# Where the first spectral products of the first half keep their operands, one values buffer, and another order of the instructions

## The chip, the core and the metric

The kernel runs on one NeuronCore of a Trainium2 chip. TensorE (PE, with its weight loads PEld) multiplies matrices into the eight PSUM banks; VectorE (DVE), ScalarE (ACT) and GpSimd (POOL) work on elements; SP issues most of the DMAs and POOL those that add to their target. The metric is the device time of one execution in microseconds; the kernel before was run three times, and its median is 233.02 us (232.19 to 233.31).

## What is computed

Two branches share the input x (2048 rows of 640 columns, bf16), and a gate mixes them:

```python
x = A_q
g = sigmoid((x * gate_w).sum(-1, keepdims=True))
# A: a 4-tap causal filter of k times v, then a long convolution by FFT along the 2048 rows
k_shift = sum(k_pad[:, t:t + S] * shift_k[:, ks - 1 - t] for t in range(ks))
kv = k_shift * v
y = irfft(rfft(kv, 2 * S) * rfft(ssm_k, 2 * S))[:S] + kv * ssm_D
a = x * y
# B: a mixer and an MLP
h = gelu(layernorm(x) @ w1)
x1 = x + shifted(h) @ w2              # four column groups, shifted by +1, -1, +2, -2 rows
b = x1 + gelu(layernorm(x1) @ w3) @ w4
out = g * a + (1 - g) * b
```

## The kernel before

All of SBUF that the kernel uses is one array, `arena`, cut into regions by hand (lines 530 to 546), and PSUM is another, `PSall`. Every instruction is recorded as an operation with the byte ranges that it reads and writes; dependencies follow from the ranges. Two long lists then fix the rest: `SEQUENCE` is the order in which the recorded operations are issued (each engine takes its own operations in this order and waits in order), and `PLACES` is the PSUM bank of each PSUM tile. `emit` turns the dependencies into semaphore waits. So an operation that is not ready holds everything behind it on its engine, DMA queues included. In the profile nearly all operations have the line of a recording helper: 646 is every matmul of `mm`, 636 every ACT operation, 626 every tensor_tensor, 631 every tensor_scalar, 238 every plain DMA, 235 every transposing DMA.

The mixer goes by four chunks of 512 rows: `x_load`, `ln1` (layer norm, transposes), `mm1` with gelu into `hT`, `mm2` by tiles of 128 rows, `ln2` (normalise, then a transposing DMA on SP), `mm3` with gelu into `uT` (12 tiles of 5 matmuls of 512 columns), `mm4` (two halves of 12 or 13 matmuls of 320 columns for a tile). `base` scales the residual rows and stores them, and `mm4` overwrites the rows in SBUF and adds them to the output by an accumulating DMA of POOL.

The convolution goes by five chunks of 128 channels. `h_load`, `h_fold`, `h_chunk` bring the filter into the frequency domain, in `HF`. `kv_load` (line 771) brings 128 channels of keys and of values with transposing DMAs, into one key buffer `kT` and one of two value buffers `vT`. `kv_chunk` (line 776) works on DVE: four scalings and three sums for the taps, the product with the values, a reversed copy on ACT, and four folds of 1024 elements; then a transposing DMA writes `xet`. `x_fwd` (line 789) transforms `xet` with 12 matmuls on PE, and ACT copies the result into `XF`, whose first index is the half (channels 0 to 319 and 320 to 639). The first half is complete after chunk 2, the second after chunk 4.

Rows are four blocks of 512. `combine(g, b)` (line 959) makes sums and differences of neighbouring blocks in `XF`: the sum (frequencies 0 and 1 of the four groups) by an accumulating DMA of POOL, the difference on DVE. `unit(hh, c)` (line 965) makes output block c of half hh: products of `XF` block c - a with `HF` block a, for a = 0 to c, each for a real and an imaginary accumulator, as operations of 2560 elements. The products of a = 1 are added by accumulating DMAs, the others on DVE. Two subtractions or sums of 1280 elements a block write the result over `XF`. `final` (line 1004) transforms back with 8 matmuls and one flip on PE, copies on ACT, and finishes on DVE; the result is added to the output by a DMA of POOL or, for the last four, stored by SP.

The buffers of `unit` come from a list, `ubuf` (line 576): regions `oYX` and `oPT` (two), the end of `oHT`, and the end of `oKV`. `oKV`, `oYX` and `oPT` lie behind one another, 15376 elements, and the chunks of keys and values use all of them: keys at 0, the first value buffer at 2064, the taps at 4112 and 6160, the reversed copy at 8208, the second value buffer at 9232, the folds (`xf2`) at 11280 and `xet` at 13328. `G`, the matrix of the back transform, is loaded over the key buffer.

Of the kernel before, what the change touches and what calls it, by code (L numbers as in the profile page):

```python
# [422 lines left out]
def bass_gated_mix__ssm_conv_h3__mixer_s_mlp__prompt_kernel(  # L423
# [32 lines left out]
    def ps(n, cls):  # L456
# [3 lines left out]
    SEQUENCE = [74, 11, 54, 76, 56, 1, 12, 7, 73, 9, 2, 53, 0, 13, 75, 14, 156, 15, 157, 16, 80, 57, 217, 17, 81, 66,  # L460
# [310 lines left out]
    def kv_load(c):  # L771
        cs = slice(128 * c, 128 * (c + 1))
        P.dma(sp, kT[:, 16:16 + S], A_k[0, :, cs], transpose=True)
        P.dma(sp, vT[c % 2], A_v[0, :, cs], transpose=True)
# [190 lines left out]
    def unit(hh, c):  # L965
# [35 lines left out]
        if c == 3:  # L1001
            pool.insert(0, V(oHF + 10240 * hh + 7680, 2560))
# [146 lines left out]
```

## Time and profile before

| What | Before |
|---|---|
| median of three runs | 233.02 us |
| the profiled execution's own time | 234.02 us |
| its span, first to last instruction | 232.2 us |
| PE, DVE, ACT, POOL busy | 218.2, 204.9, 175.4, 91.7 us |
| PEld busy | 128.2 us |
| granted TensorE clock, mean | 0.993 |
| DMA packets, bytes | 81439, 46.00 MB |

Busy times are unions of instructions on one engine; matmuls are pipelined and their ends are modelled, so a busy PE is not PE at its peak, but a gap in it is a wait. A row of a timeline gives the start, the length, the engine, the line, the operation, what it writes and reads, and in brackets the idle time before it with what ended it; instructions of one line that follow each other are merged under the shape of the first. A stretch of the windows view gives start and end, its length, then busy microseconds (and instructions) of PE, PEld, DVE, ACT and POOL, the granted clock, the DMA engines' share and GB/s. Times are microseconds from the span's start.

### The profile page before, as it was taken

What the parts mean: (1) busy time and instruction counts of PE and PEld (TensorE: products, weight loads), DVE (VectorE), ACT (ScalarE), POOL (GpSimd) and SP (SyncE); (2) the same over time, 40 slices, a digit from 0 to 9 for tenths busy, and PEclk for the clock granted to TensorE, in tenths of its full rate; (3) what the DMA queues carried; (4) which work ended last, traced back from release to release, by engine and by line L of the source; (5) the groups of instructions that cost most, each with busy time, mean ns of one, the idle gap of its engine ahead of it and who ended that gap; (6) DMA issues with size and microseconds to landing.
All of it is one profiled execution on the core that took longest, in us unless ns stands there. A gap on an engine that the chain in (4) does not pass through costs nothing.

```text
span 232.2 us, 3873 instructions
## 1 busy us (share of the span) xinstructions
PE 218.2 (94%) x1426; PEld 128.2 (55%) x1437; DVE 204.9 (88%) x336; ACT 175.4 (76%) x315; POOL 91.7 (40%) x114
## 2 busy tenths in 40 slices
PE   7998999999999999987999989999999999999970
PEld 2486866555545634434665437654577554777640
DVE  4999997999799999695556997999999999999993
ACT  2197996796899979987877995458983869446990
POOL 0335140324214000372115814595128634636890
PEclk9999999999999999999999999999999999999997
DMA  6999999999999999999999999999899999899997
GB/s 174 320 233 311 132 247 232 202 203 207 233 142 263 182 229 223 296 210 223 179 203 173 163 163 200 198 189 183 165 249 203 182 224 151 159 173 111 112 138 142
DMA packets 81439, 46.00 MB, mean 198 GB/s; under 512 B 60024, under 2 KB 75916, under 8 KB 81420
## 3 DMA queue, kind: packets, MB, share of 16 engines
q1 hardware_dynamic: 71560, 31.92, 64.5%
q0 software_dynamic: 9696, 13.77, 38.3%
q8 instruction: 11, 0.18, 0.3%
q10 hardware_dynamic: 164, 0.07, 0.1%
q14 instruction: 8, 0.07, 0.1%
HBM read 14.92 MB, written 6.55 MB: 92 GB/s over the span
## 4 chain that ended last, share of the span: by engine, by line
PE 80%; ACT 9%; DMA 5%; DVE 4%; issue 1%
PE PSall L646 74%; ACT arena L636 9%; DMA arena<-arena 5%; DVE arena L626 3%; PE PSall L674 3%; PE PSall L678 2%; PE PSall L865 1%; DVE arena L918 0%; DVE arena L670 0%; PE PSall L709 0%
## 5 line engine op out<-in xcount | busy, mean ns | idle before, releaser
L646 PE MATMUL PSall<-arena 128*128 128x320 bf16 (+5 forms) x1345 | 206.1, 309 | 6.4 <-ACT arena L636 3.1
L646 PEld LDWEIGHTS PSall<-arena 128*128 128x128 bf16 (+1 forms) x1354 | 121.9, 98 | 90.4 <-ACT arena L636 7.5
L626 DVE TENSOR_TENSOR arena<-arena 128x2560 bf16<-128x2560 bf16 (+6 forms) x195 | 158.5, 865 | 13.5 <-DMA arena<-arena 4.7
L636 ACT ACTIVATE arena<-PSall 128x512 bf16<-128x512 f32 (+7 forms) x182 | 104.8, 630 | 23.1 <-PE PSall L646 15.1
L636 ACT ACTIVATE arena<-arena 128x640 bf16<-128x640 bf16 (+4 forms) x75 | 54.0, 747 | 11.0 <-DVE arena L626 6.9
L238 POOL DMA_DIRECT2D out_dram<-arena x28 | 29.3, 1141 | 20.8 <-ACT arena L636 15.5
L238 POOL DMA_DIRECT2D arena<-arena x18 | 20.4, 1131 | 37.7 <-DVE arena L626 23.4
L636 ACT ACTIVATE arena<-PSall,arena 128x640 bf16<-128x640 f32 (+1 forms) x32 | 20.4, 658 | 15.4 <-PE PSall L646 15.2
L814 POOL TENSOR_TENSOR arena<-arena 128x1 f32<-128x1 f32 (+2 forms) x17 | 18.7, 1104 | 29.1 <-DVE arena L825 20.6
L631 DVE TENSOR_SCALAR arena<-arena 128x640 bf16<-128x640 bf16 (+3 forms) x45 | 23.7, 541 | 1.2 <-DMA arena<-arena 0.4
L626 POOL TENSOR_TENSOR arena<-arena 128x4 bf16<-128x4 bf16 (+3 forms) x26 | 15.9, 675 | 21.3 <-DVE arena L626 14.5
L631 POOL TENSOR_SCALAR arena<-arena 128x2 f32<-128x2 f32 (+4 forms) x21 | 11.0, 527 | 25.6 <-DVE arena L811 8.7
L810 DVE BATCH_NORM_STATS2 arena<-arena 128x6 f32<-128x320 bf16 x32 | 14.4, 483 | 2.1 <-DMA arena<-in_A_q_dram 2.0
L918 DVE SCALAR_TENSOR_TENSOR arena<-PSall,arena 128x640 bf16<-128x640 f32 x12 | 9.8, 822 | 3.6 <-PE PSall L646 3.6
L674 PE MATMUL PSall<-arena 128*128 128x512 bf16 x15 | 6.1, 594 | 1.6 <-DVE arena L670 1.6
L678 PE MATMUL PSall<-arena 128*128 128x512 bf16 x24 | 6.6, 379 | 0.0
L674 PEld LDWEIGHTS PSall<-arena 128*128 128x128 bf16 x15 | 2.1, 143 | 5.1 <-issue 3.6
L865 PE MATMUL PSall<-arena 128*128 128x128 bf16 x40 | 3.3, 219 | 0.1
L678 PEld LDWEIGHTS PSall<-arena 128*128 128x128 bf16 x26 | 2.4, 98 | 1.6
L865 PEld LDWEIGHTS PSall<-arena 128*128 128x128 bf16 x40 | 2.7, 98 | 0.6
L636 ACT ACTIVATE PSall<-PSall 128x640 f32<-128x640 f32 x4 | 2.8, 688 | 0.1
L811 DVE BATCH_NORM_AGGREGATE arena<-arena 128x2 f32<-128x12 f32 x16 | 2.7, 192 | 0.0
(26 smaller groups left out, 10.8 us busy)
## 6 DMA issues: line engine op xcount, KB each, us to landing
arena<-arena POOLq DMA_DIRECT2D x12, 640.0 KB, 6.6
arena<-in_A_q_dram SPq DMA_DIRECT2D x14, 320.0 KB, 4.8
out_dram<-arena POOLq DMA_DIRECT2D x20, 160.0 KB, 4.5
arena<-in_A_ssm_k_dram SPq DMA_DIRECT2D x5, 512.0 KB, 5.8
arena<-in_B_w_dram SPq DMA_DIRECT2D x4, 480.0 KB, 4.7
arena<-arena POOLq DMA_DIRECT2D x6, 320.0 KB, 4.5
out_dram<-arena SPq DMA_DIRECT2D x10, 160.0 KB, 4.5
arena<-in_B_w_dram SPq DMA_DIRECT2D x1, 1152.0 KB, 7.0
```

The costliest lines, as they stand in the source:

```text
L238: fn = lambda e: e.dma_start(out, in_, **kw)
L626: P.op(eng, lambda e: e.tensor_tensor(o, real(a), real(b), op), [a, b], [o], dve_ns(o, [a, b], 2) if eng == "dve" else 500)
L631: P.op(eng, lambda e: e.tensor_scalar(o, real(a), s1, s2, op0=op0, **({} if op1 is None else {"op1": op1})), [a] + aps, [o], dve_ns(o, [a] ...
L636: P.op("act", lambda e: e.activation(real(o), real(a), f, bias=bias, scale=scale, **({"accum_out": accum} if accum is not None else {})), ...
L646: fns.append(lambda e, l=l, r=r, i=i: e.matmul(real(o), l, r, start=(i == 0), stop=(i == last)))
L674: P.op("pe", lambda e: e.matmul(real(pw), warm[:, 0:128], warm[:, 128:640], start=True, stop=True), [warm], [pw], 427.0 if i < 14 else 216.0)
L678: P.op("pe", lambda e: e.matmul(real(pw), warm[:, 0:128], warm[:, 128:640], start=True, stop=True), [warm], [pw], 216.0)
L810: P.op("dve", lambda e, o=o, i=i: e.bn_stats(o, i), [i], [o], 400)
L811: P.op("dve", lambda e: e.bn_aggr(bna[:, t, :], bns[k]), [bns[k]], [bna[:, t, :]], 120)
L814: P.op("pool", lambda g: g.tensor_tensor(o, a, e, ALU.pow), [a, e], [o], dur)
L865: P.op("pe", [lambda e, c=c, pb=pb, xn=xn: e.transpose(real(pb)[:, 128 * c:128 * (c + 1)], xn[:, 128 * c:128 * (c + 1)], ident) for c in r ...
L918: P.op("dve", lambda e: e.scalar_tensor_tensor(x, real(pr), 1.0, x, op0=ALU.mult, op1=ALU.add, accum_out=st[1, 0][:, t:t + 1]), [pr, x], [ ...
```

## The change

The regions are used in another way, and the two lists are other ones.

- The chunks of keys and values now lie in the first 12304 elements: one value buffer, the reversed copy over it, the folds at 8208 and `xet` at 10256. So the values load of a chunk must wait until the chunk before has read its reversed copy.
- The first two units of the first half (blocks 3 and 2) take three buffers: the end of `oHT`, `oW2` (the weights of `mm2`, which are spent by then), and the end of the old `oPT` (offset 12816 behind `oKV`), which the chunks do not touch. From unit (0,1) on, three buffers inside `oKV` follow in place of `oW2`, where `final` keeps its results.
- With three buffers, these two units add each product as it comes: a = c down to 1, into one temporary (real part) and into `XF`'s own block (imaginary part), whose values are spent after the first two products. The products of a = 1 are still added by DMA. The number of products and of sums is the same.
- `combine` of the first half makes its sums on DVE in place of POOL's DMA.
- `SEQUENCE` and `PLACES` are others throughout. Around the last two chunks of keys and values the order is now as follows.
  - SP: values of chunk 3, transpose of chunk 2's folds, a part of w4, keys of chunk 4, two parts of w4, an `ln2` transpose, transpose of chunk 3's folds, the last part of w4, an `ln2` transpose, values of chunk 4, two `ln2` transposes, G, seven `base` stores, transpose of chunk 4's folds. Before: values of chunk 3, transpose of chunk 2's folds, two parts of w4, keys of chunk 4, two parts of w4, values of chunk 4, transpose of chunk 3's folds, two `base` stores, two `ln2` transposes, three `base` stores, transpose of chunk 4's folds, and G later.
  - DVE: chunk 3, then chunk 4 with six combine operations and the first three products of unit (0,3) among its own; its other nine products and sums follow at once, then products of units (0,2) and (0,1). Before: chunk 3, chunk 4 with one combine operation of the first half in it, and unit (0,3) behind it.
  - PE: six tiles of `mm3(0)`, `x_fwd(2)`, the other six tiles, nine of the 12 matmuls of `x_fwd(3)`, then `mm4` of tiles 0 to 3 with the other three among them, three tiles of `mm3(1)`, four matmuls of `x_fwd(4)`, nine more tiles of `mm3(1)` with two matmuls of `x_fwd(4)` between the last two, the other six matmuls, and `mm4` of tiles 4 to 7. The first back transforms, of block 3, stand before and after the last half of these, ahead of `mm3(2)`; before, the first ones came after it.
  - At the start the first two tiles of x are loaded in the other order, and the weights of `mm1` earlier.

The diff, without the two lists:

```diff
-    kT, vT = V(oKV, 2064), [V(o, 2048) for o in (oKV + 2064, oKV + 9232)]
+    kT, vT = V(oKV, 2064), V(oKV + 2064, 2048)
     tap = [V(oKV + 4112 + 2048 * i, 2048) for i in range(2)]
-    xrev = V(oKV + 8208, 1024).rearrange("p (b h n) -> p b h n", b=4, h=2)
+    xrev = V(oKV + 2064, 1024).rearrange("p (b h n) -> p b h n", b=4, h=2)
...
-    xf2 = V(oKV + 11280, 2048).rearrange("p (e a b n) -> p e a b n", e=2, a=2, b=4)
-    xet = V(oKV + 13328, 2048).rearrange("p (e b c) -> p e b c", e=4, b=4)
+    xf2 = V(oKV + 8208, 2048).rearrange("p (e a b n) -> p e a b n", e=2, a=2, b=4)
+    xet = V(oKV + 10256, 2048).rearrange("p (e b c) -> p e b c", e=4, b=4)
...
-    ubuf = [V(o, 2560) for o in (oYX, oPT, oPT + 2560, oHT + 7680, oKV + 5120)]
+    first = [V(o, 2560) for o in (oHT + 7680, oW2, oKV + 12816)]
+    later = [V(oKV + o, 2560) for o in (5120, 7680, 10240)]
...
-        P.dma(sp, vT[c % 2], A_v[0, :, cs], transpose=True)
+        P.dma(sp, vT, A_v[0, :, cs], transpose=True)
...
     def combine(g, b):
-        P.dma("pool", XF[:, g, b, 0:2].rearrange("p j r d -> p (j r d)"), XF[:, g, b - 1, 0:2].rearrange("p j r d -> p (j r d)"), accum=True)
+        if g:
+            P.dma("pool", XF[:, g, b, 0:2].rearrange("p j r d -> p (j r d)"), XF[:, g, b - 1, 0:2].rearrange("p j r d -> p (j r d)"), accum=True)
+        else:
+            tt(XF[:, g, b, 0:2], XF[:, g, b, 0:2], XF[:, g, b - 1, 0:2], ALU.add)
         tt(XF[:, g, b, 2:4], XF[:, g, b, 2:4], XF[:, g, b - 1, 2:4], ALU.subtract)
...
-        if c:
+        few = not hh and c > 1
+        if few:
+            T = pool.pop(0)
+            for a in range(c, 0, -1):
+                for o, t, r in ((R, T, 0), (I, Xc, 1)):
+                    prod(t, a, r)
+                    if a > 1:
+                        tt(o, o, t, ALU.add)
+                    else:
+                        P.dma("pool", o.rearrange("p (i n) -> p i n", i=2), t.rearrange("p (i n) -> p i n", i=2), accum=True)
+            pool.append(T)
+        elif c:
...
-        if c > 1:
+        if c > 1 and not few:
...
+        if few and c == 2:
+            pool[:] = later + [b for b in pool if b.offset != first[1].offset]
```

More of the change, by code (lines that the diff above doesn't have):

```diff
@@ L458, in ps @@
         return v if n == 1 else v.rearrange("p (b n) -> p b n", b=2)
[L460 removed]
[59 rows of a table removed]
[L521 removed]
[5 rows of a table removed]
+    SEQUENCE = [76, 11, 56, 74, 54, 9, 1, 12, 75, 5, 4, 53, 7, 13, 8, 0, 73, 10, 14, 156, 15, 157, 16, 57, 60, 17, 81,
[59 rows of a table added]
+    PLACES = [0, 7, 2, 1, 1, 3, 4, 4, 5, 6, 2, 1, 0, 5, 6, 3, 7, 5, 5, 7, 0, 4, 7, 6, 1, 3, 7, 2, 6, 0, 4, 2, 7, 4, 6,
[5 rows of a table added]
     HW = S + 4
@@ L783, in kv_chunk @@
                 tt(kv, kv, dst[j], ALU.add)
-        tt(kv, kv, vT[c % 2], ALU.mult)
+        tt(kv, kv, vT, ALU.mult)
         q = kv.rearrange("p (b h n) -> p b h n", b=4, h=2)
@@ L959, in combine @@
     def combine(g, b):
-        P.dma("pool", XF[:, g, b, 0:2].rearrange("p j r d -> p (j r d)"), XF[:, g, b - 1, 0:2].rearrange("p j r d -> p (j r d)"), accum=True)
+        if g:
+            P.dma("pool", XF[:, g, b, 0:2].rearrange("p j r d -> p (j r d)"), XF[:, g, b - 1, 0:2].rearrange("p j r d -> p (j r d)"), accum=True)
+        else:
+            tt(XF[:, g, b, 0:2], XF[:, g, b, 0:2], XF[:, g, b - 1, 0:2], ALU.add)
         tt(XF[:, g, b, 2:4], XF[:, g, b, 2:4], XF[:, g, b - 1, 2:4], ALU.subtract)
-    pool = list(ubuf)
+    pool = list(first)
     def unit(hh, c):
@@ L1109, in bass_gated_mix__ssm_conv_h3__mixer_s_mlp__prompt_kernel @@
         at(unit, 1, c)
-    spare = sorted((b.offset for b in pool if b.offset in (oYX, oPT, oPT + 2560, oHT + 7680)), key=[b.offset for b in pool].index)[0]
+    spare = sorted((b.offset for b in pool if b.offset in [a.offset for a in first + later[1:]]), key=[b.offset for b in pool].index)[0]
     abl = [V(spare + 640 * i, 640).rearrange("p (e d) -> p e d", e=2) for i in range(4)]
```

1 line of the change is left out of this document (removed), and 128 rows, old and new, of tables (PLACES, SEQUENCE).

## The prediction

> **What bounds the kernel now.** I read the page's busy times and chain first, then TensorE's idle time by stretch, then the timelines of the engines where that idle time lies. The busy times, the DMA slices and the chain by engine:
>
> ```profile
> span 232.2 us, 3873 instructions
> PE 218.2 (94%) x1426; PEld 128.2 (55%) x1437; DVE 204.9 (88%) x336; ACT 175.4 (76%) x315; POOL 91.7 (40%) x114
> ...
> DMA  6999999999999999999999999999899999899997
> ...
> PE 80%; ACT 9%; DMA 5%; DVE 4%; issue 1%
> ```
>
> TensorE (PE) is busy for 94% of the span and is 80% of the chain. The change takes no matmul away, so it can win only what PE waits, plus what follows the last matmul. The 16 DMA engines are busy nearly throughout. Busy time by stretch (start:end, length, then busy us of PE, PEld, DVE, ACT, POOL):
>
> ```profile
> 20.00:30.00 10.00, 8.60 (x95) 7.09 (x94) 9.55 (x23) 9.72 (x29) 4.18 (x7) 1.00 1.22 192
> ...
> 100.00:110.00 10.00, 7.73 (x45) 4.24 (x45) 7.18 (x9) 7.87 (x14) 4.51 (x8) 1.00 1.17 194
> ...
> 120.00:130.00 10.00, 9.73 (x55) 5.13 (x54) 7.51 (x8) 8.07 (x15) 5.64 (x5) 1.00 0.97 195
> 130.00:140.00 10.00, 9.31 (x46) 4.29 (x45) 9.93 (x9) 9.86 (x18) 4.16 (x7) 1.00 0.92 152
> 140.00:210.00 70.00, 70.00 (x447) 43.39 (x446) 68.04 (x71) 46.08 (x83) 36.31 (x33) 1.00 1.01 190
> ...
> 220.00:232.20 12.20, 5.24 (x35) 3.16 (x33) 8.13 (x25) 6.39 (x13) 5.95 (x5) 0.87 0.97 137
> ```
>
> From 140 to 210 PE has no idle time: nothing can be won there, only lost. Between 100 and 140 it idles 2.27 + 0.27 + 0.69 = 3.2 us (110 to 120 has next to none). The early 1.40 us (20 to 30) and the tail after 216 remain. PE's timeline names the middle waits:
>
> ```profile
> 104.53 3.57 PE L646 MATMUL PSall<-arena 128*128 128x320 bf16 x25 [0.69 <-ACT arena L636]
> 109.69 13.12 PE L646 MATMUL PSall<-arena 128*128 128x512 bf16 x82 [1.58 <-DMA arena<-arena]
> 123.08 15.32 PE L646 MATMUL PSall<-arena 128*128 128x512 bf16 x75 [0.27 <-ACT arena L636]
> 139.09 3.16 PE L646 MATMUL PSall<-arena 128*128 128x320 bf16 x22 [0.69 <-ACT arena L636]
> ```
>
> The 1.58 us is `x_fwd` of chunk 3, waiting for the transpose of that chunk's folded values. The 0.69 at 104.53 and at 139.09 are the first `mm4` behind an `mm3`, waiting for the last gelu. VectorE (DVE) idles far more in the same stretch:
>
> ```profile
> 96.42 0.68 DVE L626 TENSOR_TENSOR arena<-arena 128x1024 bf16<-128x1024 bf16 x1
> ...
> 106.45 1.23 DVE L626 TENSOR_TENSOR arena<-arena 128x2048 bf16<-128x2048 bf16 x1 [1.59 <-DMA arena<-in_A_v_dram]
> 108.80 4.88 DVE L626 TENSOR_TENSOR arena<-arena 128x1024 bf16<-128x1024 bf16 x6 [1.12 <-ACT arena L636]
> 118.38 3.02 DVE L626 TENSOR_TENSOR arena<-arena 128x2560 bf16<-128x2560 bf16 x2 [4.70 <-DMA arena<-arena]
> 123.72 2.23 DVE L626 TENSOR_TENSOR arena<-arena 128x2560 bf16<-128x2560 bf16 x2 [2.32 <-PE PSall L646]
> ...
> 144.24 0.16 DVE L825 SCALAR_TENSOR_TENSOR arena<-arena 128x1 f32<-128x1 f32 x1 [1.40 <-ACT arena L636]
> ...
> 173.91 54.55 DVE L626 TENSOR_TENSOR arena<-arena 128x2560 bf16<-128x2560 bf16 x86
> ```
>
> These waits sum to 11.1 us; then DVE runs practically unbroken to 228.46, so it ends the kernel. The 4.70 us is the first product of `unit(0,3)`, whose buffers still held the last chunk's folds until their transpose had read them. That is what the own buffers remove.
>
> **The change part by part.** *DVE.* The units' products and sums are the same number of 2560-element operations as before. Three `combine(0,b)` halves move from POOL's DMA to DVE:
>
> ```profile
> L626 DVE TENSOR_TENSOR arena<-arena 128x2560 bf16<-128x2560 bf16 x52 | 75.4, 1486 | 7.6 <-DMA arena<-arena 4.7 <-PE PSall L646 2.3 <-ACT arena L636 0.2
> L626 DVE TENSOR_TENSOR arena<-arena 128x1280 bf16<-128x1280 bf16 x22 | 17.4, 819 | 0.0
> L626 DVE TENSOR_TENSOR arena<-arena 128x2048 bf16<-128x2048 bf16 x20 | 24.5, 1223 | 1.9 <-DMA arena<-in_A_v_dram 1.6
> L631 DVE TENSOR_SCALAR arena<-arena 128x2048 bf16<-128x2048 bf16 x20 | 14.9, 748 | 0.7 <-DMA arena<-in_A_k_dram 0.4
> ```
>
> That is 3 x 0.82 = 2.5 us of DVE. Against the 11.1 us of waits that early products can fill, DVE could be up to 8.6 us ahead of today from about 145 on. PE cannot follow: its matmuls stay, so DVE's lead is worth only PE's waits and part of the tail. The 2.5 us are hidden by that lead; with the cover gone they would stand in full at the end.
>
> *The third chunk's transpose (1.58 + 0.69 us).* SP and POOL around it:
>
> ```profile
> 91.25 4.15 SPq L235 DMA_TRANSPOSE arena<-in_A_k_dram  x1
> 95.45 1.11 SPq L238 DMA_DIRECT2D arena<-in_B_w_dram  x2
> 96.60 4.94 SPq L235 DMA_TRANSPOSE arena<-in_A_v_dram  x1
> 101.64 4.20 SPq L235 DMA_TRANSPOSE arena<-arena  x1
> ...
> 119.29 1.22 SPq L235 DMA_TRANSPOSE arena<-arena  x1
> ```
>
> ```profile
> 98.22 1.11 POOL L238 DMA_DIRECT2D arena<-arena  x1
> 106.44 0.92 POOL L238 DMA_DIRECT2D arena<-arena  x1 [3.41 <-DMA arena<-arena]
> 111.44 0.91 POOL L238 DMA_DIRECT2D arena<-arena  x1 [3.51 <-DMA arena<-arena]
> ```
>
> ```profile
> arena<-arena POOLq DMA_DIRECT2D x6, 320.0 KB, 4.5
> ...
> out_dram<-arena SPq DMA_DIRECT2D x12, 80.0 KB, 3.1
> ...
> arena<-arena SPq DMA_TRANSPOSE x30, 4.2
> ...
> arena<-in_A_v_dram SPq DMA_TRANSPOSE x5, 6.3
> ```
>
> The folds are done at 96.42 + 0.68 = 97.1, but the transpose stands behind the last chunk's values load and issues only at 101.64; PE gets it at 109.69, 8.05 us later, where the median transpose lands after 4.2. The three accumulating copies of `combine` (98.22, 106.44, 111.44) run beside it and the next one. In the new order the transpose comes before the values load, behind the key load, two weight loads and one small transpose: 91.25 + 4.15 + 1.11 + 1.22 (a small transpose, as at 119.29) = 97.7, so it issues near 98. It lands between 98 + 4.2 = 102.2 and 98 + 8.05 = 106.1. PE now has the rest of `mm3-0` first and needs it where `mm3-0` ends, at 104.53 - 0.69 = 103.8. The wait is 0 to 2.2 us; since the copies beside it are gone I stay near the low end, 0.7. `mm4` then stands behind nine matmuls of `x_fwd`, which cover the gelu wait. Gain: 2.27 - 0.7 = **1.5 us** (bounds 0 to 2.3).
>
> The Trainium skill, page "DMA: Bandwidth & Descriptors", section "Issuing engines are not separate DMA queues", says that transfers of SP and POOL share the same 16 engines and interleave. The 8.05 against 4.2 us agree with it; by that rule taking the copies away brings the low end, without it the transpose keeps 8.05 and the gain here is near nothing.
>
> *The last chunk's transpose.* Between 97.1 and it DVE now has chunk 4 (4 scalings of 0.75, 4 operations of 1.22, 4 folds of 0.68: 10.6), six combine halves (4.9) and three products (4.5): 20.0, so 117.1, with half a microsecond of waits 117.6. It lands at 121.8 to 125.7. PE needs it where it has done chunk 3, four `mm4` and 15 matmuls of `mm3-1`; today `mm3-1` begins 13 matmuls into the burst at 123.08; at 3.57 / 25 = 0.14 us each, near 124.9.
>
> ```profile
> 126.00:137.00 11.00, 11.00 (x53) 1.00 0.96 154
> ```
>
> At 11.00 / 53 = 0.21 us a matmul the 15 add 3.2, the 12 of chunk 4 that are now later take off 2.5, the gains above and the 0.27 take off 1.8: 123.8. The wait is 0 to 1.9; I take 0.5, against today's 0.27: **-0.2 us**.
>
> *The wait at 139.09.* Six matmuls of `x_fwd(4)` now stand between the last `mm3-1` and `mm4-6`, 1.3 us, more than the 0.69 us gelu wait: **+0.7 us**.
>
> *The single values buffer.* The load of chunk c+1 waits for chunk c's second fold, and while it waits it holds all that follows on SP. For chunk 4 it comes behind the transpose, at about 102 to 103, and lands by its median 6.3 us later, at 109; DVE multiplies by it 12.7 us of queue after 97.1 plus some waits, near 110.5. Hidden, by 1.5 us. If it lands like today's (issued at 96.60, DVE released at 106.45, 9.85), it lands at 112.5 and DVE stops for 2 us. The matrix G, which takes the key buffer, stands behind it on SP until DVE has read the keys, near 109, and ahead of the `base` stores, whose rows ACT's `mm4` overwrites. They land 3.1 us later, near 113; the first whole `mm4` tile leaves PE after ten matmuls of `x_fwd(3)` and five halves of 12 or 13, near 104.5 + 2.1 + 61 x 0.14 = 115. Covered by 2 us.
>
> The Trainium skill, page "Trainium Kernel Development and Optimization", section "Best Practices", advises two buffers so that loads overlap computing, which speaks against this edit. Here DVE already waited 1.59 us with two, because the load's place on SP decided; the rule's price is the 2 us above.
>
> *The start.* Tiles, fills and weight loads are reordered. PE's 1.40 us between 20 and 30 can go or double; nothing there is removed, and the first statistics begin on the tile that is now loaded second. I charge **-0.3 us** (bounds -1.4 to +1.4).
>
> *The tail.* DVE's last 12 us stay the same operations. Today it enters them late because it is behind; with the lead PE sets their start. PE's share of the tail stays. I take **+0.2 us** of at most 1.4.
>
> Sum: 1.5 - 0.2 + 0.7 - 0.3 + 0.2 = **1.9 us**. The profiled execution took 234.02, 1.82 more than its span of 232.2 and 1.0 more than the median. Span 230.3, execution 232.1, median 233.02 - 1.9 = **231.1 us**, own range 230.0 to 231.9.
>
> **The rivals.** *Slower: the DMA engines stay the limit.* If the transpose of chunk 3 keeps 8.05 us, it lands at 106.1 and PE waits 2.2, so 1.5 of the gain is lost. The values load comes behind it on SP: 98 + 4.20 + 0.55 of a weight load + 1.22 = 104.0, and 9.85 later it is 113.9. DVE stops from 110.5 on, 3.4 us; the last transpose issues at 117.6 + 3.4 = 121.0 and lands at 129.0, where PE stands at 123.8 + 1.5 = 125.3. That is 3.7 us of wait in place of 0.5: 231.1 + 1.5 + 3.2 = **235.8**. It makes the kernel slower by over 0.5% once the last transpose lands after 127.4. For it: DMA slices of 9 throughout, and the load's own 9.85. Against: the copies are gone from just this stretch.
>
> *Same: the unbroken stretch breaks.* From 140 to 210 PE never waits. The first inverse transforms now stand ahead of `mm3-2`, 60 matmuls or 12.6 us sooner, and `ln2` of the last tile issues its ACT operation only some 36 matmuls of `mm4` (5.0 us) ahead of `mm3-3`:
>
> ```profile
> L636 ACT ACTIVATE arena<-arena 128x640 bf16<-128x640 bf16 x40 | 32.8, 834 | 4.1 <-POOL arena L626 3.6 <-DMA arena<-arena 0.5
> ```
>
> ACT's 0.83, SP's 1.22 and a landing of 4.2 (taken from the issue's start, so 5.0 to 6.3 in all) cost PE 0 to 1.3 us there, and as much again where DVE, ACT and PE hand a transform on: 231.1 + 1.3 + 1.3 = **233.7** at most, 232.4 with one of them. Against it: DVE is ahead there.
>
> *Faster still: all middle waits go and DVE's lead shows in the tail*: 2.3 in place of 1.5, 0.3 in place of -0.2, 0.7, and 1.2 of the tail, less 0.3 at the start, is 4.2: near **228.9**. For it the 11.1 us; against it, every landing must be early.
>
> *It does not do what it says:* the early products wait for ACT's evacuation of `x_fwd(2)`, which the new order mixes with gelus. DVE then gains no lead and carries 2.5 us more: 235.5, within the slower case.
>
> **How the numbers follow.** Forecast 0.42, faster still 0.13, same 0.18, slower 0.27 (0.20 for the DMA case, 0.07 for the products and other waits). About 0.5% (1.2 us) is what a measurement can tell from no change: faster 0.55, same 0.18, slower 0.27. The range 229.0 to 235.0 leaves out the best part of the fast case and the worst of the slow one.
>
> **What would show it.** DVE's 4.70 us wait gone, and products between the folds of chunk 4. The folded transpose of chunk 3 issued near 98 and PE's wait for it under 1 us. No gelu wait ahead of the second block of `mm4`. PE still unbroken from 140 to 210. Wrong, if the last values load holds DVE, if PE waits over 2 us for the last transpose, or if new waits of PE lie before 100.

## The result, and the profile after

The changed kernel takes 231.38 us (median of 20 executions, 230.54 to 235.74) against 233.21 us for the kernel before beside it; the ratio is 0.9935, interval 0.9908 to 0.9962. A second set gave 231.05 against 233.02, ratio 0.9915 (0.9887 to 0.9943). The gain is 1.8 to 2.0 us by the medians and 1.5 to 2.0 by the ratios; 1.9 was forecast. Ratios leave out executions over 1.5% above the fastest of their kernel; medians and ranges do not.

The profiled execution took 233.02 us with a span of 231.2, so it is one of the longer ones; what it has that others lack comes out below. Its busy times:

```profile
span 231.2 us, 3878 instructions
PE 219.1 (95%) x1437; PEld 127.0 (55%) x1437; DVE 206.8 (89%) x339; ACT 175.3 (76%) x315; POOL 96.3 (42%) x111
```

The stretches of the prediction from 100 on, with the same columns:

```profile
100.00:110.00 10.00, 10.00 (x58) 5.51 (x57) 9.97 (x12) 9.77 (x18) 0.00 (x0) 1.00 1.01 200
...
120.00:130.00 10.00, 10.00 (x49) 4.54 (x48) 9.90 (x7) 8.13 (x12) 5.26 (x5) 1.00 0.89 147
130.00:140.00 10.00, 10.00 (x60) 5.52 (x59) 9.75 (x8) 6.88 (x13) 4.79 (x5) 1.00 1.17 190
140.00:210.00 70.00, 67.87 (x429) 41.75 (x428) 65.22 (x74) 48.09 (x85) 40.10 (x36) 1.00 1.00 185
```

From 100 to 140 PE is now busy throughout; before it idled 2.27 + 0.27 + 0.69 = 3.2 us there. All four middle waits are gone. But from 140 to 210, where nothing was lost before, 70.00 - 67.87 = 2.13 us are. PE's timeline has one wait there:

```profile
178.43 36.76 PE L647 MATMUL PSall<-arena 128*128 128x320 bf16 x234 [2.13 <-ACT arena L637]
```

VectorE in the middle, and SP:

```profile
95.53 2.62 DVE L627 TENSOR_TENSOR arena<-arena 128x1024 bf16<-128x1024 bf16 x4 [2.55 <-ACT arena L637]
...
107.72 9.17 DVE L627 TENSOR_TENSOR arena<-arena 128x1280 bf16<-128x1280 bf16 x10
...
117.02 18.68 DVE L627 TENSOR_TENSOR arena<-arena 128x2560 bf16<-128x2560 bf16 x13
```

```profile
94.66 6.39 SPq L235 DMA_TRANSPOSE arena<-arena  x2
...
102.97 2.67 SPq L235 DMA_TRANSPOSE arena<-in_A_v_dram  x1
...
116.96 2.27 SPq L235 DMA_TRANSPOSE arena<-arena  x1
```

Lines of the kernel are one higher than before. DVE's 4.70 us wait is gone, as are the 1.59 for the values and the 2.32 for PE: ten operations run without a gap from 107.72 (a tap sum, the product with the values, folds, combine halves and the early products), and thirteen more from 117.02. On SP the second of the two transposes merged at 94.66 is chunk 3's; it issues at 98.2, the last chunk's at 116.96. The `DMA to landing` line of the source view, for each of them alone:

```profile
L235 SPq DMA_TRANSPOSE arena<-arena x1: 2864/2864/2864, 98.2 to 98.2; - x1
DMA to landing us min/median/max: 4.3/4.3/4.3
```

```profile
L235 SPq DMA_TRANSPOSE arena<-arena x1: 2271/2271/2271, 117.0 to 117.0; - x1
DMA to landing us min/median/max: 4.6/4.6/4.6
```

Both land near the median, and PE waits for neither.

### The profile page after: what moved, and what is told of

It reads as the page before. It is cut to its first block, busy times and chain, and to the rows that moved or that the text cites. A ratio compares the mean times of both kernels' runs of the same rounds, so it can differ in the third digit from the quotient of the medians.

```text
span 231.2 us, 3878 instructions
## 1 busy us (share of the span) xinstructions
PE 219.1 (95%) x1437; PEld 127.0 (55%) x1437; DVE 206.8 (89%) x339; ACT 175.3 (76%) x315; POOL 96.3 (42%) x111
## 4 chain that ended last, share of the span: by engine, by line
PE 77%; ACT 11%; POOL 5%; DVE 4%; issue 2%
PE PSall L647 71%; ACT arena L637 10%; DVE arena L627 3%; POOL arena L627 3%; PE PSall L679 2%; PE PSall L675 2%; POOL arena L238 1%; POOL arena L815 1%; ACT PSall L637 1%; PE PSall L866 1%; DVE arena L919 0%; POOL out_dram L238 0%; DVE arena L671 0%; PE PSall L710 0%
## 5 line engine op out<-in xcount | busy, mean ns | idle before, releaser
L647 PE MATMUL PSall<-arena 128*128 128x320 bf16 (+4 forms) x1354 | 206.1, 310 | 4.9 <-ACT arena L637 3.0
L627 DVE TENSOR_TENSOR arena<-arena 128x2560 bf16<-128x2560 bf16 (+6 forms) x198 | 161.1, 864 | 11.4 <-ACT arena L637 9.6
L647 PEld LDWEIGHTS PSall<-arena 128*128 128x128 bf16 x1354 | 120.5, 98 | 90.5 <-ACT arena L637 10.3
L637 ACT ACTIVATE arena<-PSall 128x512 bf16<-128x512 f32 (+8 forms) x182 | 106.1, 628 | 26.4 <-PE PSall L647 18.2
L238 POOL DMA_DIRECT2D out_dram<-arena x28 | 32.6, 1300 | 46.4 <-ACT arena L637 37.9
L627 POOL TENSOR_TENSOR arena<-arena 128x4 bf16<-128x4 bf16 (+3 forms) x26 | 23.2, 915 | 25.2 <-DVE arena L627 24.5
L238 POOL DMA_DIRECT2D arena<-arena x15 | 22.2, 1490 | 23.9 <-DVE arena L627 23.9
L815 POOL TENSOR_TENSOR arena<-arena 128x1 f32<-128x1 f32 (+2 forms) x17 | 17.9, 1054 | 20.3 <-DVE arena L826 10.8
L632 POOL TENSOR_SCALAR arena<-arena 128x2 f32<-128x2 f32 (+4 forms) x21 | 11.9, 571 | 13.4 <-DVE arena L812 6.1
L675 PE MATMUL PSall<-arena 128*128 128x512 bf16 x15 | 5.5, 551 | 1.6 <-DVE arena L671 1.6
L679 PE MATMUL PSall<-arena 128*128 128x512 bf16 x26 | 6.6, 379 | 0.0
L675 PEld LDWEIGHTS PSall<-arena 128*128 128x128 bf16 x15 | 1.9, 134 | 4.7 <-issue 2.8
L866 PEld LDWEIGHTS PSall<-arena 128*128 128x128 bf16 x40 | 2.6, 98 | 1.3 <-ACT arena L637 0.4
L679 PEld LDWEIGHTS PSall<-arena 128*128 128x128 bf16 x26 | 2.2, 97 | 1.7
```

The lines of the kernel that those rows point to most:

```text
L238: fn = lambda e: e.dma_start(out, in_, **kw)
L627: P.op(eng, lambda e: e.tensor_tensor(o, real(a), real(b), op), [a, b], [o], dve_ns(o, [a, b], 2) if eng == "dve" else 500)
L632: P.op(eng, lambda e: e.tensor_scalar(o, real(a), s1, s2, op0=op0, **({} if op1 is None else {"op1": op1})), [a] + aps, [o], dve_ns(o, [a] ...
L637: P.op("act", lambda e: e.activation(real(o), real(a), f, bias=bias, scale=scale, **({"accum_out": accum} if accum is not None else {})), ...
L647: fns.append(lambda e, l=l, r=r, i=i: e.matmul(real(o), l, r, start=(i == 0), stop=(i == last)))
L675: P.op("pe", lambda e: e.matmul(real(pw), warm[:, 0:128], warm[:, 128:640], start=True, stop=True), [warm], [pw], 427.0 if i < 14 else 216.0)
```

## The experiments

Each kernel ran beside the kernel before on the same chip; the kernel before had medians of 233.02 to 233.26 us there, so medians are compared across chips too. The theory: two things held the transposes back in the kernel before, their place on SP and the copies of POOL beside them; PE's waits there were what could be won, and DVE's early work is cover and no more. The rivals are told with each run.

### The changed kernel again: is the wait at 178 part of it?

No edit.

> The changed kernel once more, without an edit. In its first profile PE waits 2.1 us ahead of mm4 of tile 9 at 178, behind ACT, which waits for one POOL product of 128x1 that took 5.91 us. Theory: that product is stretched now and then by DVE's two-input products beside it, and such executions are the ones near 233.5, the others lie near 231. So an execution near 231 shows the product at 1 to 2 us and no PE wait over 1 us between 140 and 210, and one near 233 shows both again. Rival: the order makes the wait, and POOL's time has nothing to do with it: the wait of about 2 us is there also with the product at 1 us.

It took 231.24 us, span 229.5. Its PE, and its POOL against that of the first profile, around 171:

```profile
84.58 130.71 PE L647 MATMUL PSall<-arena 4*128 4x512 bf16 x781 [0.25 <-issue]
```

```profile
170.87 1.27 POOL L627 TENSOR_TENSOR arena<-arena 128x1 f32<-128x1 f32 x1
```

```profile
170.83 5.91 POOL L627 TENSOR_TENSOR arena<-arena 128x1 f32<-128x1 f32 x1
```

The second fence is this run, the third the first profile: one program, the same instruction, 1.27 and 5.91 us. It is the last product of `ln_math` for tile 15. In the first profile ACT's `ln2` waits for it, and behind `ln2` in ACT's order stands the copy that frees the PSUM bank for the next `mm4`:

```profile
176.78 0.92 ACT L637 ACTIVATE arena<-arena 128x640 bf16<-128x640 bf16 x1 [3.22 <-POOL arena L627]
177.60 0.77 ACT L637 ACTIVATE arena<-PSall,arena 128x640 bf16<-128x640 f32 x1
```

With the product at 1.27 us PE has no wait from 84.58 to 215. The 0.25 us ahead of 84.58 is no wait either: this profile records 1425 matmuls of 1437, and a weight load at 84.25 has no matmul behind it; the first profile, which records all 1437, has that matmul and no gap. So the 2.13 us belong to that execution, not to the order; they are more than the whole 1.78 us between the two times.

### The same product on ACT

```diff
-            tt(s[4], s[2], s[5], ALU.mult, eng="pool")
+            if a < 12:
+                tt(s[4], s[2], s[5], ALU.mult, eng="pool")
+            else:
+                act(s[4], s[2], ACTF.Copy, scale=s[5])   # placed right ahead of its ln2
```

> The changed kernel with the last product of ln_math of tiles 12 to 15 (one element for each partition) on ACT, right ahead of the ACT operation that needs it, in place of POOL. Theory (POOL's product beside DVE's two-input products makes the wait at 178): the wait of 2.1 us is gone, PE is busy for over 69.3 of the 70 us from 140 to 210, the times come in one group near 230.6 to 231.2, and the long group near 233.5 is gone. Rival (ACT's own queue is late there, and POOL is only seen as the releaser): PE still waits 1 to 2 us near 178, and the times are those of the changed kernel. Second rival (POOL's power operation is stretched just as the product was): the wait moves to the power operation and stays over 1 us.

231.07 us (six executions, 230.91 to 231.81), ratio 0.9917 (0.9886 to 0.9947). PE is busy for 70.00 of 70 us from 140 to 210. That agrees with the theory, but the run before has shown that the same holds without the edit. So both kernels were timed once more, side by side.

> The changed kernel without an edit, timed beside the next one, for the share of long executions. Theory: one part near 230.5 to 231.9 and a smaller one (a fifth to a third) from 233 on, as among its first 20 times. Rival (the long ones were chance of that chip): all below 232.5.

> The changed kernel with ln_math's last product of tiles 12 to 15 on ACT once more, for the share of long executions. Theory (the stretched POOL product makes them): no execution above 232.5, median 230.8 to 231.3, 0.2 to 0.6 us below the changed kernel on the same chip. Rival: long executions as often as in the changed kernel; then the POOL product is one way to be late among others.

The changed kernel: 231.05 us (nine, 230.59 to 232.00). With the product on ACT: 231.28 us (seven, 230.74 to 231.86), ratio 0.9914 (0.9883 to 0.9945). No difference. In the first set 6 of 20 executions of the changed kernel lay above 232.5, here none of nine: the rival (chance) held for this chip. So the edit's worth can't be told, and that the stretched product made all the six long ones isn't shown; one profile shows one of them.

### The combine sums by DMA again

```diff
-        if g:
-            P.dma("pool", ...accum=True)
-        else:
-            tt(XF[:, g, b, 0:2], XF[:, g, b, 0:2], XF[:, g, b - 1, 0:2], ALU.add)
+        P.dma("pool", ...accum=True)
```

> The changed kernel with the three sums of combine(0, b) as accumulating DMAs of POOL again, at the same places of the order. Theory (the copies held the transposes back, as the forecast had it): the transposes of the last two chunks land 1 to 4 us later, PE waits 1 to 2.5 us in all between 100 and 125, DVE saves 2.5 us, the time is 1 to 2 us longer than that of the changed kernel. Rival (the place on SP alone did it): the transposes land as in the changed kernel, PE waits under 0.3 us there, and the time is the same within 0.5 us. Either way the first product of unit(0,3) waits for a DMA in place of a DVE instruction, by up to 3.5 us of DVE.

232.55 us (ten, 231.48 to 233.16), ratio 0.9977 (0.9951 to 1.0003): 1.2 us more than the changed kernel by the medians and 1.0 by the ratios, as the theory had it, but not by its way. Chunk 3's transpose issues at 98.2 and lands 4.3 us later, as in the changed kernel, and PE waits 0.46 us between 100 and 125. The first copy issues at 101, behind that transpose, and no longer beside it. What changes is DVE, which waits for a copy in the first product:

```profile
107.55 1.49 DVE L627 TENSOR_TENSOR arena<-arena 128x2560 bf16<-128x2560 bf16 x1 [2.38 <-DMA arena<-arena]
...
118.33 23.00 DVE L627 TENSOR_TENSOR arena<-arena 128x2560 bf16<-128x2560 bf16 x16
```

It is at 118.33 where the changed kernel is at 117.02, 1.3 us later although it has three operations less to do. The profile shows 0.2 to 0.9 us of the 1.2 (span 229.7, against 229.5 and 228.8 of the changed kernel's second and third profiles); it took 231.48, the lowest of the ten, and the rest stays open.

### The values load ahead of the transpose again

```diff
+    SEQUENCE.remove(705); SEQUENCE.insert(SEQUENCE.index(691), 705)   # values of chunk 4 ahead of chunk 3's transpose
```

> The changed kernel with the last chunk's values load put back on SP ahead of the transpose of chunk 3's folds. Theory (that place on SP is what made PE wait): the load must wait for chunk 3's second fold in the single buffer and takes 2.7 to 5 us of SP, so the transpose issues at 100.5 to 103 in place of 98, PE waits 1.5 to 3 us for it near 104, and the time grows by 1 to 2.5 us. Rival (DMA load decides when it lands, the issue does not): the transpose is seen by PE as before and the time stays within 0.5 us.

231.49 us (eight, 230.83 to 232.98), ratio 0.9930 (0.9902 to 0.9959): nothing that can be measured. The load took 3.09 us of SP; the transpose issued at 100.1, 1.9 us later, and landed 4.4 us after that. PE:

```profile
104.51 2.12 PE L647 MATMUL PSall<-arena 128*128 128x512 bf16 x9 [0.26 <-DMA arena<-arena]
106.96 108.21 PE L647 MATMUL PSall<-arena 128*128 128x320 bf16 x677 [0.33 <-issue]
```

0.26 + 0.33 us are lost, where 1.5 to 3 were expected. In the new order the place on SP alone makes PE wait no more than that.

### Both undone

The two edits above, in one kernel:

```diff
+        P.dma("pool", ...accum=True)   # the sums of combine(0, b)
+    SEQUENCE.remove(705); SEQUENCE.insert(SEQUENCE.index(691), 705)
```

> The changed kernel with both undone: the three sums of combine(0, b) by POOL's DMA and the last values load ahead of chunk 3's transpose. Alone, the first cost 1.2 us of time and left that transpose's landing at 102.3, the second cost 0.1 to 0.2 us and moved it to 104.2 with 0.6 us of PE. Theory (each spoils what the other leaves, since a copy now lies beside the transpose): it lands at 105 to 108, PE waits 1.5 to 3.5 us for it, and the time is 2 to 3.5 us longer than that of the changed kernel. Rival (they only add): it lands near 104.2, PE loses 0.6 to 1.1 us there, and the time is 1.2 to 1.6 us longer.

235.55 us (ten, 233.24 to 239.05), ratio 1.0074 (1.0039 to 1.0110). They do not add: 1.2 and 0.1 us alone, 4.2 together by the medians (235.55 - 231.38), 3.2 by the ratios (0.0139 x 233); by the ratios the size is the theory's. The way is not. The transpose lands 4.3 us after 99.7, so at 104.0, and PE does not wait for it. It waits later:

```profile
108.39 115.40 PE L647 MATMUL PSall<-arena 128*128 128x320 bf16 x726 [2.23 <-issue]
```

The instruction at 108.39 is the first `mm4`, which reads all four parts of w4. The last part is the DMA behind the transpose on SP, issued at 101.8 in this run, with a 320 KB copy of POOL issued at 101.2 beside it; in the changed kernel it issues at 101.1 and lands 4.3 us later, at 105.4, before the first `mm4`. By the semaphore events it lands at 108.3 in this run, 6.5 us after its issue, and at 106.9 in the run above, 4.5 us after its issue at 102.35 with no copy beside it; in both the first `mm4` starts within 0.1 us of that. So "issue", the name for a wait that the profile shows no cause for, was a late load of w4 in these two runs. The profiled execution took 233.24, the lowest of the ten; why the others lie 2 us above it is open.

### The sums on DVE, alone, in the kernel before

```diff
 # in the kernel before
-        P.dma("pool", ...accum=True)
+        if g: P.dma("pool", ...accum=True)
+        else: tt(XF[:, g, b, 0:2], XF[:, g, b, 0:2], XF[:, g, b - 1, 0:2], ALU.add)
```

> The kernel before with one part of the change alone: the three sums of combine(0, b) on DVE, at their old places of the order. Theory (the copies fill the DMA engines beside the last transposes): the transpose of chunk 3, issued near 101.4 as before, reaches PE 1 to 3 us sooner and PE's wait of 1.58 us there goes to under 0.5 us; DVE takes 2.5 us more, which lie partly in its waits of 11 us; the time is 0 to 1.5 us shorter. Rival (SP's place decides): PE's wait stays at 1.3 to 1.8 us, and the time is the same or up to 2 us longer by DVE's 2.5 us.

233.17 us (ten) against 233.13, ratio 1.0009 (0.9979 to 1.0038). The last values load, in the kernel before and in this one:

```profile
L235 SPq DMA_TRANSPOSE arena<-in_A_v_dram x1: 4942/4942/4942, 96.6 to 96.6; - x1
DMA to landing us min/median/max: 9.8/9.8/9.8
```

```profile
L235 SPq DMA_TRANSPOSE arena<-in_A_v_dram x1: 4174/4174/4174, 95.9 to 95.9; - x1
DMA to landing us min/median/max: 6.2/6.2/6.2
```

Without the copies it lands in 6.2 in place of 9.8 us, and PE's wait of 1.58 us is gone. PE is busy for 38.22 us from 100 to 140, 1.5 more than before. All of it is given back at the end, where PE waits for DVE; in the first fence the kernel before, in the second this run:

```profile
224.70 0.72 PE L646 MATMUL PSall<-arena 128*128 128x320 bf16 x2 [0.39 <-DVE arena L626]
225.93 0.31 PE L646 MATMUL PSall<-arena 128*128 128x320 bf16 x1 [0.51 <-DVE arena L626]
```

```profile
221.47 2.08 PE L646 MATMUL PSall<-arena 128*128 128x320 bf16 x14 [0.19 <-DVE arena L626]
224.92 0.45 PE L646 MATMUL PSall<-arena 128*128 128x320 bf16 x2 [1.38 <-DVE arena L626]
226.16 0.31 PE L646 MATMUL PSall<-arena 128*128 128x320 bf16 x1 [0.79 <-DVE arena L626]
```

0.90 us of waits became 2.36. DVE's added 2.5 us are not what does it: DVE starts its last long run at 172.78, 1.1 us sooner than in the kernel before (173.91), which then has no wait of DVE. Here two follow:

```profile
220.85 2.43 DVE L626 TENSOR_TENSOR arena<-arena 128x320 bf16<-128x320 bf16 x8 [0.40 <-ACT arena L636]
224.18 4.49 DVE L626 TENSOR_TENSOR arena<-arena 128x320 bf16<-128x320 bf16 x12 [0.91 <-DMA out_dram<-arena]
```

The second is for an output DMA of POOL, which stands on POOL behind a wait for earlier ones. POOL issued the last of these 1.1 us sooner than in the kernel before (212.03 against 213.15), and by the semaphore events it landed at the same time (216.34 and 216.47). So in this execution the landings of output DMAs took what the transposes gave; why they didn't come sooner is open.

The transpose of chunk 3 itself, by the semaphore events: in the kernel before, issued at 101.64 beside the first copy, it landed 7.8 us later; here, issued at 100.21 with no copy, 4.3 us later.

### The transpose first, alone, in the kernel before

```diff
+    SEQUENCE.remove(705); SEQUENCE.insert(SEQUENCE.index(691) + 1, 705)   # in the kernel before
```

> The kernel before with another part alone: on SP the transpose of chunk 3's folds ahead of the last values load. Theory (place and copies together): it issues near 97.7 in place of 101.4, PE sees it before it needs it and the wait of 1.58 us is under 0.4 us; but the values load, issued near 102 and landing 6 to 10 us later, comes after the 105 at which DVE has its taps, so DVE waits 3 to 7 us in place of 1.59, the last transpose issues 2 to 5 us later, and PE waits 2 to 4 us for it near 123: the time is the same or 1 to 2 us longer. Rival (DVE has room enough): no PE wait near 123 over 1 us, and the time is 1 to 2 us shorter.

234.64 us (ten, 234.01 to 243.01), ratio 1.0070 (1.0033 to 1.0108): slower by 1.5, in the theory's range. The wait of 1.58 us for the transpose is gone, but PE waits 1.22 us for an evacuation of ACT at 111.47 in its place; DVE waits 2.60 us for the values (1.59 before), less than the 3 to 7 expected, and PE has no wait over 0.3 us near 123. The transpose, issued at 98.46 beside the first copy (98.40), landed 6.9 us later, at 105.3, before PE asked for it at 110.2. So the place decides when it issues and the copies how long it takes, and in the old order a change of either alone ends PE's wait. What was won at 109.69 was lost again at 111.47, and PE's last two waits for DVE grew from 0.90 to 1.76 us (0.97 + 0.79). The profile (234.53, against 234.02 of the kernel before's) shows 0.5 us of the 1.5; the rest is open.

### The products late, without an own buffer

```diff
-    first = [V(o, 2560) for o in (oHT + 7680, oW2, oKV + 12816)]
-    later = [V(oKV + o, 2560) for o in (5120, 7680, 10240)]
+    first = [V(o, 2560) for o in (oKV + 7680, oW2, oKV + 12816)]
+    later = [V(o, 2560) for o in (oKV + 5120, oHT + 7680, oKV + 10240)]
...
+    SEQUENCE: 773, 775, 776 (products of unit(0,3)) right behind 719 (the last chunk's transpose)
```

> The changed kernel with the early products undone: the first accumulator of unit(0,3) and unit(0,2) lies over the last chunk's folds (two of the buffers change places), and the three products that stood among chunk 4's folds stand behind the last fold. Nothing else moves. Theory (DVE's lead is worth only what PE waits): the last chunk's transpose issues 4.5 us earlier, near 112.5; DVE then waits 4 to 5 us for it and has lost that much of its lead from 117 on; PE stays busy for over 69 of the 70 us from 140 to 210, and the time grows by 0 to 1 us. Rival (DVE has no lead to lose; the own buffers are the gain): DVE's 4 to 5 us come through to the end, at the transforms behind mm3 or in the tail, and the time grows by 3 to 5 us.

240.94 us (four), ratio 1.0332 (1.0277 to 1.0387): 9.6 us above the changed kernel, beyond even the rival.

```profile
122.32 4.42 DVE L627 TENSOR_TENSOR arena<-arena 128x2560 bf16<-128x2560 bf16 x3 [6.90 <-DMA arena<-arena]
```

```profile
131.21 1.03 PE L647 MATMUL PSall<-arena 128*128 128x512 bf16 x2 [6.82 <-ACT arena L637]
```

Two things were not foreseen. The transpose did not issue at 112.5 but at 117.22, since it writes `xet`, and the last matmul of `x_fwd(3)`, which reads it, stands among `mm4` and ends at 117.2. And a small DVE operation of `ln_math` (tiles 8 to 11) stood behind the waiting product; ACT's `ln2` waited 8.20 us for what follows from it, and PE for ACT. The next run takes this second thing away.

### The same, behind that small operation

```diff
-    773, 775, 776 right behind 719
+    773, 775, 776 right behind 507 (the operation of ln_math)
```

> As the kernel with the late products (one accumulator over the last folds, three products behind the last fold), but the small operation of ln_math of tiles 8 to 11 stands ahead of them on DVE. In that kernel it stood behind the waiting product, ACT's ln2 and so mm3 waited for it, and PE lost 6.8 us. Theory (that place in the queue was the cost): the 6.8 us PE wait near 131 is gone, DVE still waits 5 to 7 us for the transpose near 122, and PE's work covers most of that: the time is 0 to 3 us above the changed kernel's. Rival (DVE has no lead to lose): DVE, which has 9 to 10 us less done at 122 and only some 3 us of waits from there to 165, shows as waits of PE for it from 140 on or at the end, and the time is 5 to 7 us above.

241.17 us (four), ratio 1.0340 (1.0295 to 1.0384). The wait at 131 is gone, and the time is the same: the theory's 0 to 3 us fall, and the rival's 5 to 7 are exceeded. DVE, PE and ACT:

```profile
122.62 8.75 DVE L627 TENSOR_TENSOR arena<-arena 128x2560 bf16<-128x2560 bf16 x6 [5.33 <-DMA arena<-arena]
```

```profile
154.06 78.27 PE L647 MATMUL PSall<-arena 128*128 128x320 bf16 x479 [7.77 <-ACT arena L637]
```

```profile
152.63 0.47 ACT L637 ACTIVATE arena<-arena 1x320 bf16<-1x320 bf16 x1 [15.56 <-DVE arena L627]
153.01 1.00 ACT L637 ACTIVATE arena<-PSall 128x1024 bf16<-128x1024 f32 x1
```

DVE does the three products now at 122.62 and comes to the thirteen that follow at 127.1, in place of 117.02. ACT's copy of one row (1x320) closes `unit(0,3)`: it waits for all of that unit's DVE work. Behind it in ACT's order stands the evacuation of `x_fwd(4)` (128x1024), and PE waits for its bank. In the changed kernel the same copy waits too, and PE doesn't notice:

```profile
141.03 0.47 ACT L637 ACTIVATE arena<-arena 1x320 bf16<-1x320 bf16 x1 [4.13 <-DVE arena L627]
```

### Own buffers, but the products late

```diff
+    SEQUENCE: 773, 775, 776 right behind 507; buffers as changed
```

> The changed kernel with its own buffers, but the three early products behind the last fold and behind that small operation of ln_math, so that only their place among the folds is undone. Theory (own buffers take the wait away, the place among the folds fills only DVE's waits there): DVE does not wait for the transpose, loses 1.5 to 2.5 us of waits between the folds, the last transpose issues no sooner than 116 (it waits for the last matmuls of x_fwd(3)), and the time is within 0.7 us of the changed kernel's. Rival (the place among the folds carries the gain): the time is 1.5 to 3 us longer.

234.77 us (ten, 233.91 to 235.78), ratio 1.0068 (1.0036 to 1.0101): 3.7 us above the changed kernel on the same chip. The rival held, and by more than it said. DVE does not wait for the transpose but loses its work between the folds:

```profile
112.64 2.62 DVE L627 TENSOR_TENSOR arena<-arena 128x1024 bf16<-128x1024 bf16 x4 [2.15 <-ACT arena L637]
117.13 0.16 DVE L826 SCALAR_TENSOR_TENSOR arena<-arena 128x4 f32<-128x4 f32 x1 [1.87 <-ACT arena L637]
```

2.15 + 1.87 = 4.0 us of waits, which the changed kernel fills with the early products. The copy of one row ends its wait at 145.32 in place of 141.03, 4.3 us later, and PE's waits begin:

```profile
146.75 1.80 PE L647 MATMUL PSall<-arena 128*128 128x320 bf16 x12 [0.46 <-ACT arena L637]
149.18 15.18 PE L647 MATMUL PSall<-arena 128*128 128x320 bf16 x81 [0.63 <-ACT arena L637]
...
226.44 0.31 PE L647 MATMUL PSall<-arena 128*128 128x320 bf16 x1 [0.60 <-DVE arena L627]
```

The last matmul starts at 226.44; in the changed kernel's second timed set it starts at 223.14:

```profile
222.23 0.31 PE L647 MATMUL PSall<-arena 128*128 128x320 bf16 x1 [0.84 <-DVE arena L627]
223.14 0.31 PE L647 MATMUL PSall<-arena 128*128 128x320 bf16 x1 [0.60 <-DVE arena L627]
```

So of the 4.3 us by which DVE is late, 3.3 reach the end. The early products among the folds are worth 3.7 us in the new order, the own buffer that spares DVE the wait another 241.17 - 234.77 = 6.4 (the clock's share, told last, in it).

## Why the prediction was right, and where it was wrong

**The bound and the sum.** That PE's waits were what could be won held: 3.2 us of them from 100 to 140 are gone, and the time fell by 1.8 to 2.0. Between the kernel before's profile and the second one of the changed kernel the last matmul comes 2.78 us sooner (225.93 and 223.15). Of the waits that can be read, the middle gave 3.2 us, the start 0.4 and the tail -0.5, where 2.0, -0.3 and 0.2 were forecast; the 0.3 us between 3.1 and 2.78 are not placed.

So the profiles give about 0.9 us more than the forecast, and that its total of 1.9 met the medians is in part luck. The waits were read in an execution of 234.02 us, 0.8 above the median of the twenty (233.21). In it the 1.58 us hang on one late part of the transpose: of the 16 semaphore events with which each DMA here ends, 15 had come by 107.84, before PE's work ahead of it ended at 108.10, and the last came at 109.41. Whether other executions of the kernel before have this wait isn't shown, and the two one-part runs in the kernel before, which lose this wait and win no time, don't tell either.

**Chunk 3's transpose (1.5).** It gave the whole 2.27. Issue near 98: 98.2. Landing 102.2 to 106.1: 102.5, the low end. The wait of 0.7 us was 0. The prediction's reason, that copies beside it had held it back, is right for the kernel before (its landing took 7.8 us with the copies and 4.3 without, that of the load ahead of it 9.8 and 6.2). But undoing the copies or the place in the new order brings no such wait back (0.26 us at most): the copies issue 3.0 and 1.5 us behind the transpose there, and its landing stays at 4.3 to 4.4 us. What is spoilt there is the last part of w4 and DVE. The rule of the Trainium skill, page "DMA: Bandwidth & Descriptors", section "Issuing engines are not separate DMA queues", that transfers of SP and POOL share engines, agrees with the 7.8 and 4.3 us.

**The last chunk's transpose (-0.2).** Issue 117.6: 116.96. It landed 4.6 us later, and the wait of 0.5 us was 0: 0.27 us gained. The working missed that the transpose could not go before 116.9 whatever DVE does, because `xet` is still read until then: the last matmul of `x_fwd(3)` ends at 116.84 and DVE's last fold at 116.89.

**The gelu wait (+0.7).** Gone, 0.69 us.

**The single values buffer (hidden by 1.5).** Hidden. By the semaphore events the values landed at 109.2, 109.7 and 109.4 in the three profiles, and DVE multiplied by them at 110.3, so the margin is 0.6 to 1.1 us; where the product of 1.49 us ahead of them was taken away, DVE waited 0.38 us. The Trainium skill, page "Trainium Kernel Development and Optimization", section "Best Practices", advises two buffers so that loads overlap computing; here DVE did not wait for the one.

**The start (-0.3) and the tail (+0.2).** Two stretches of the first profile of the changed kernel, which has all matmuls on record, then the second of them in the kernel before:

```profile
20.00:30.00 10.00, 9.79 (x109) 7.82 (x107) 9.74 (x26) 9.79 (x27) 2.77 (x7) 1.00 1.25 206
30.00:50.00 20.00, 19.11 (x109) 9.93 (x107) 18.93 (x37) 17.52 (x35) 10.64 (x15) 1.00 1.04 235
```

```profile
30.00:50.00 20.00, 19.89 (x149) 11.60 (x152) 18.05 (x36) 16.54 (x32) 6.46 (x10) 1.00 1.11 216
```

From 20 to 30 the loss went from 1.40 to 0.21 us, from 30 to 50 it grew from 0.11 to 0.89: 0.4 won, where 0.3 was charged. Two waits for ACT, 0.33 us at 33.4 and 0.56 at 47.1, are new, so the sign "new waits of PE before 100" that the prediction named against itself did come, though the start as a whole lost nothing. The tail's sign was wrong: PE's last two waits for DVE are 0.84 + 0.60 us in place of 0.39 + 0.51, 0.5 us lost where 0.2 was to be won.

**DVE's lead: the step that failed.** The lead over the kernel before came as forecast: the work that DVE still has ahead of it at 145 is 82.4 us in the kernel before and 74.0 in the second profile of the changed kernel, 8.4 us less (8.6 was the bound). What failed is the step from lead to cover, "The 2.5 us are hidden by that lead". With the late products of the last run DVE has 78.0 us left at 145, still 4.4 us ahead of the kernel before, and the time is 1.7 us longer than that kernel's (234.77 against 233.02). For the new order has moved forward what waits for DVE as well, ACT's one-row copy of `unit(0,3)` with the evacuations behind it and the first inverse transforms. In the kernel before that copy stands later than in both, and PE doesn't wait:

```profile
146.56 0.47 ACT L636 ACTIVATE arena<-arena 1x320 bf16<-1x320 bf16 x1 [2.36 <-DVE arena L626]
```

In the new order 4.3 us of lateness there cost 3.3 at the end, so about 1 us is spare, not 8.6. The sum wasn't hurt because DVE came in time: in the second and third profiles PE has no wait at all from 85 to 221. The rival "it does not do what it says" (235.5) comes near the run with late products (234.77) by its "no lead"; its cause, products that wait for ACT's evacuation of `x_fwd(2)`, did not arise.

**The rivals.** "Slower" did not come; both of its conditions (transpose at 8.05, load at 9.85) were gone. "Same" named the right stretch and the wrong cause: the profiled execution did lose 2.13 us between 140 and 210, at an `ln2` of the last tile, but behind a stretched POOL product and not the landing, and ahead of `mm4`, not of `mm3-3`; in the second and third profiles that stretch has no wait.

## What to carry to other kernels

When an engine that doesn't set the time fills its idle time with later work, the lead it gains is slack only as long as nothing that depends on it is moved forward too: find the instruction on another engine that relays its lateness (here a copy of one row ahead of PSUM evacuations in ACT's order) and read how long it waits. Parts of a change that cost 1.2 and 0.1 us to undo alone cost 3 to 4 us when undone together here, so test them in pairs as well. And one profile shows one execution: look at a second one before a wait, new or old, is explained by the kernel.

## What the runs showed of the hardware

The same POOL product of one element for each partition took 1.27 us in two profiles of the changed kernel and 5.91 in one, in each beside DVE's run of two-input products. The Trainium skill, page "SBUF — State Buffer", section "Who interferes with whom", says that DVE's second pair of ports is the only one GpSimd has, held exclusively, which would let a DVE that runs without gaps keep POOL out. But DVE's run there is the same in all three profiles (16.57 us from 170.3 or 170.4 on), so it alone doesn't decide, and the run with that product on ACT cannot bear it out, since the wait did not come in the kernel beside it either; so this is argued, not shown.

A long wait of PE was paid twice. The stretches behind the 6.8 us wait that ended at 131 (late products), then the one that holds the end of the 7.8 us wait at 154 (late products behind the small operation); the granted clock is the third number from the end:

```profile
130.00:135.00 5.00, 3.53 (x8) 1.01 (x9) 5.00 (x4) 4.42 (x7) 2.30 (x4) 0.50 0.74 98
135.00:140.00 5.00, 5.00 (x22) 2.15 (x21) 4.90 (x5) 2.75 (x5) 2.75 (x3) 0.87 0.89 153
```

```profile
150.00:160.00 10.00, 5.94 (x23) 3.40 (x24) 9.83 (x10) 5.20 (x9) 6.53 (x7) 0.51 0.93 194
```

The granted clock was at half for several microseconds around the end of these two waits; the waits of 2.13 us (first profile) and 2.23 us (both undone) left it at 1.00. In the second of these kernels the last matmul starts at 234.08, 10.9 us later than in the changed kernel (223.14). 7.77 us of that are the wait; an estimate for the clock, 5.94 us of work at 0.51 and so some 3 us lost, gives the rest.
